# Block 0's out product over four token groups at once, with unit 2 inside it, and the batch rests moved to block 6

## The chip, the core and the metric

The kernel runs on one core of a Trainium2 chip. A core has a matmul engine (TensorE, PE), an elementwise engine (VectorE, DVE), an engine for activations and copies (ScalarE, ACT), a general one (GpSimd, POOL) and a queue engine (SyncE, SP) which here only issues DMA transfers. All five run their own instruction lists in order and wait for one another by semaphores. Matmuls write to PSUM, eight banks of 512 floats in each of 128 partitions; everything else lies in SBUF. The metric is the device time of one execution in microseconds. One execution is also profiled, instruction by instruction; its own time and its span (first to last instruction) are given beside the median.

## What is computed

Chunked attention (chunks of 64 positions, no mask, heads of 64), then a bilinear feed-forward network. Inputs and output are float32.

```python
batch, n_heads, seq, head_dim = (8, 8, 576, 64)
n_tokens, d_model, d_ff = (4608, 512, 1536)
...
q_c = q.reshape(B, H, nc, chunk, D)
k_c = k.reshape(B, H, nc, chunk, D)
v_c = v.reshape(B, H, nc, chunk, D)
scores = scale * np.matmul(q_c, k_c.transpose(0, 1, 2, 4, 3))
scores = scores - np.max(scores, axis=-1, keepdims=True)
attn = np.exp(scores)
attn = attn / (np.sum(attn, axis=-1, keepdims=True) + 1e-09)
out = np.matmul(attn, v_c)
...
x = np.ascontiguousarray(attn_out.transpose(0, 2, 1, 3)).reshape(B * S, H * D)
a = x @ w_a
b = x @ w_b
return (a * b @ w_out).astype(np.float32)
```

## The kernel before, in words

**Blocks and units.** The 4608 tokens are cut into nine blocks (K = 0 to 8) of 512 tokens. A block is two units (u = 2K, 2K + 1) of 256 tokens, that is four chunks of 64. A batch has 576 positions: eight chunks go to a block of their own, and the ninth chunks of all eight batches, the rests, make one more block. `REST` (L51) says which block that is: block 4 before. For the rests two neighbouring chunks come from different batches, so that `runs` (L112) gives two runs of 64 partitions where it gives one of 128 otherwise. Loads (`load_natural`, L119) and stores (`store`, L435) issue one DMA per run: four issues a tensor and unit in place of two, and two a store in place of one.

**Attention of a unit.** q, k, v are loaded into `f32` (three sets), cast to bf16 by POOL (`cast_qk`, `cast_v`; `qkb`, `vb`), and q, k are turned so that the head dimension lies on partitions (`qkT`). For units 4 and up a DMA turns them (`transpose_dma`, L216). For units 2 and 3 PE does: `load_pairs` loads two tokens a row, `cast_pairs` casts, `transpose_pairs` (L190) makes eight transposes for q or k into an F bank, `evacuate_pairs` (L199) copies them out, q by DVE, k by ACT. Then `scores` (32 small matmuls into the two banks `PS`, L234), `expo` (ACT, L245), `sums` (four matmuls of ones with the exponentials, into two F banks, L251), `values` (32 small matmuls into the two banks `PA`, L267), `log_sums` (ACT, L277), `inverse` (ACT, exp of the negative logarithm, L281) and `normalise` (DVE, L286, one for each of the two chunk halves), which writes `xT`. `slot(uv, us)` (L686) issues the sums, values and logarithms of unit uv and the scores of unit us; what follows is put in a list `late`, from which `step()` takes one item before each tile and `drain()` all.

**The network.** A tile `ffn(K, ft)` takes 128 of the 1536 columns of w_b and w_a: four matmuls for b, four for a, into two banks of a ring of four (`F`, by `nextF`, L108); ACT copies b out (L409), DVE multiplies it with a into `ab[ft]` (L410). `us` says which units' columns it takes: both (512 columns) or one (256). The out product of a token group `tg` (128 tokens) is the sum over the twelve ft of ab[ft] times w_out (`out_products`, L420); `out_close` (L428) copies it from PSUM to a buffer `osb`, and `store` writes it out. Blocks 0 and 1 do that; blocks 2 to 8 use a scheme of fewer products (`outs_fast`, L470), which needs sums of w_out halves that POOL makes on the side (`some_sums`). w_out comes in six pieces: `queue_wo(i)` issues the load, `land_wo(i)` casts it on POOL.

**Order.** The order is written out by hand: each engine works through its instructions in the order of the program text, and the DMA issues of SP likewise. Around the change it is:

1. Block 0's twelve tiles (L710 to L729). Meanwhile SP issues the loads of w_out (0 to 5), then of units 2, 3, 4.
2. POOL's casts of w_out, then of units 2 and 3 (L730 to L748).
3. Block 0's out product (L749 to L775): groups 0 and 1 together in two banks, ft by ft; then group 2 in a third bank, with unit 2's transposes after its ft 5, and unit 2's scores and exponentials after it; then group 3, with `slot(2, None)` and unit 3's transposes of q after its ft 4 and those of k after ft 7; at its end unit 3's scores.
4. Casts, w_out sums, turns and loads for the units that follow, and block 0's stores (L777 to L796).
5. Block 1 (L798 to L834). Unit 3's sums and values aren't there yet, so its first seven tiles are done in halves: first unit 2's columns (with `slot(3, None, short=True)` after ft 1), then unit 3's (with unit 4's scores after ft 2); the last five tiles take both. Then its out product.
6. Blocks 2 to 8 in one loop (L837 to L861), with a slot twice a block.

Of the kernel before, what the change touches and what calls it, by code (L numbers as in the profile page):

```python
# [11 lines left out]
def kernel(  # L12
# [10 lines left out]
    nc = tc.nc  # L23
# [14 lines left out]
    NFT = DFF // 128  # L38
    BLK = 512
    NBLK = NTOK // BLK  # L40
# [7 lines left out]
        return sb.tile(shape, dt, name=name)  # L48


    REST = NBLK // 2  # L51
    chunks = []
    for K in range(NBLK):
        if K == REST:
# [7 lines left out]
    PS = pp.tile([128, 2, 512], FP32, name="PS")  # L62
# [45 lines left out]
    def nextF():  # L108
        return ring("f", F)
# [19 lines left out]
    def load_pairs(u, x, src, eng):  # L129

        b, s0 = chunks[4 * u]
        eng.dma_start(
            out=f32[u % NF32][x].rearrange("p (h c) -> p h c", h=H),
            in_=src[b, :, s0:s0 + 256, :].rearrange("h (p r) d -> p h (r d)", r=2),
        )
# [39 lines left out]
    def cast_pairs(u, x, *engs):  # L175
        n = 2 // len(engs)
        for i, eng in enumerate(engs):
            r = slice(n * i, n * i + n)
            copy(
                eng,  # L180
                qkb[u % 2][:, x, :].rearrange("p (r h d) -> p h r d", r=2, h=H)[:, :, r],
                f32[u % NF32][x].rearrange("p (h r d) -> p h r d", h=H, r=2)[:, :, r],
            )
# [3 lines left out]
        for i in range(pieces):  # L187
            copy(eng, vb[u % 3][:, n * i:n * i + n], f32[u % NF32][2][:, n * i:n * i + n])

    def transpose_pairs(u, x):  # L190
        t = nextF()
        for n in range(8):
            c = n * 128
            nc.tensor.transpose(
                t.bitcast(BF16)[:, c:c + 128], qkb[u % 2][:, x, c:c + 128], identity
            )
        return t
# [221 lines left out]
    def out_products(tg, ft, o):  # L419
        nc.tensor.matmul(  # L420
            o,
            ab[ft][:, tg * 128:(tg + 1) * 128],
            wo[ft // 2][:, ft % 2, :],
            start=(ft == 0),
            stop=(ft == NFT - 1),
        )

    def out_close(K, tg, o, now=True):  # L428
        t = ring("o", osb)
        nc.vector.tensor_copy(out=t, in_=o)  # L430
        if now:
            store(K, tg, t)
        return K, tg, t
# [116 lines left out]
    with tc.manual_schedule():  # L550
# [36 lines left out]
        def queue_wo(i):  # L587
            staged["o", i] = load_wo(i, nc.sync)

        def land_wo(i):  # L590
            copy(G, wo[i], staged["o", i].rearrange("p (f c) -> p f c", f=2))
# [69 lines left out]
        def load_unit(u, xs=(0, 1, 2)):  # L661
            for x in once("load", u, xs):
                load_natural(u, x, (q, k, v)[x], nc.sync)

        def cast_unit(u, xs=(0, 1, 2)):
            for x in once("cast", u, xs):
                if x < 2:
                    cast_qk(u, x, G)
                else:
                    cast_v(u, G)  # L670
# [5 lines left out]
        def turn_pairs(u, x, engs):  # L676
            evacuate_pairs(u, x, transpose_pairs(u, x), engs)
# [3 lines left out]
        def drain():  # L681
            while late:
                fn, a = late.pop(0)
                fn(*a)

        def slot(uv, us, pairs=False, short=False):  # L686


            drain()
            if uv is not None:  # L690
                SU = nextF(), nextF()
                sums(uv, SU)
                values(uv)
                log_sums(uv, SU)
                if short:
                    for cl in range(2):
                        late.extend([(inverse, (uv, cl)), (normalise, (uv, cl))])
                else:
                    inverse(uv)
                    late.extend([(normalise, (uv, 0)), (normalise, (uv, 1))])  # L700
            if us is not None:
                scores(us, pairs)
                late.append((expo, (us,)))

        def step():
            if late:
                fn, a = late.pop(0)
                fn(*a)

        for ft in range(1, NFT):  # L710
            ffn(0, ft)
            if ft in (1, 2, 3, 4, 5):
                land_w(ft)
            if ft in (1, 2):
                queue_w(ft + 3)
            if ft == 3:
                for i in range(3):
                    queue_wo(i)
            if ft == 4:
                for i in range(3, 6):  # L720
                    queue_wo(i)
                load_pairs(2, 0, q, nc.sync)
                load_pairs(2, 1, k, nc.sync)
                load_unit(2, (2,))
            if ft == 5:
                load_pairs(3, 0, q, nc.sync)
                load_pairs(3, 1, k, nc.sync)
                load_unit(3, (2,))
                load_unit(4)  # L729
        for i in range(6):  # L730
            land_wo(i)
        wo_sums = [(i, part) for i in range(NP) for part in range(4)]

        def some_sums(n):

            for i, part in wo_sums[:n]:
                sum_wo(i, part, G)
            del wo_sums[:n]

        cast_pairs(2, 0, G)  # L740
        some_sums(1)
        cast_unit(2, (2,))
        cast_pairs(3, 0, G)
        cast_pairs(3, 1, G)
        some_sums(2)
        cast_unit(3, (2,))
        cast_pairs(2, 1, V, A)
        load_unit(5, (0,))  # L748
        o = nextF(), nextF()  # L749
        for ft in range(NFT):  # L750
            for tg in range(2):
                out_products(tg, ft, o[tg])
        stores = [out_close(0, tg, o[tg], False) for tg in range(2)]
        o = nextF()
        for ft in range(NFT):
            out_products(2, ft, o)
            if ft == 5:
                turn_pairs(2, 0, (V,))
                turn_pairs(2, 1, (A,))
        slot(None, 2, True)  # L760
        drain()
        stores.append(out_close(0, 2, o, False))
        o = nextF()
        for ft in range(NFT):
            out_products(3, ft, o)
            if ft == 4:
                slot(2, None)
                turn_pairs(3, 0, (V,))
                drain()
            if ft == 7:  # L770
                nextF()
                turn_pairs(3, 1, (A,))
        stores.append(out_close(0, 3, o, False))
        slot(None, 3, True)
        drain()  # L775

        cast_unit(4, (0,))  # L777
        some_sums(2)
# [6 lines left out]
        for d in stores:  # L785
            store(*d)
        load_unit(6, (0,))
        cast_unit(5, (0,))
        some_sums(3)
        cast_unit(5, (1,))  # L790
# [3 lines left out]
        turn_unit(5)  # L794
        load_unit(6, (1, 2))
        load_unit(7, (0,))  # L796

        for ft in range(7):  # L798
            step()
            ffn(1, ft, (0,))  # L800
            if ft == 1:
                slot(3, None, short=True)
        for ft in range(7):
            step()
            ffn(1, ft, (1,))
            if ft == 2:
                slot(None, 4)
# [6 lines left out]
        load_unit(7, (1, 2))  # L814
        load_unit(8, (0,))
        cast_unit(7, (0, 1))
        for ft in range(7, NFT):
            step()
            ffn(1, ft)
            if ft == 10:  # L820
                slot(4, 5)
# [70 lines left out]
```

## Time and profile before

| | |
|---|---|
| median of 6 runs | 314.98 us (313.9 to 315.84) |
| the profiled execution | 314.69 us, span 312.9 us |
| granted TensorE clock | 1.0 |
| DMA moved over the span | 55.00 MB, mean 176 GB/s |
| HBM read, written | 37.75 MB, 9.44 MB |
| turned q, k (DMA): issues, median to landing | 14, 5.2 us |
| out product of block 0, first matmul | 37.08 us |
| block 1, first matmul | 51.88 us |
| block 1, first tile over both units | 65.48 us |
| block 2, first product of the out step | 110.60 us |

How to read it: engine busy times overlap, so they don't add up to the span. A line of the timeline gives start, duration, engine, source line, operation, what it writes from what, and in brackets how long the engine had stood before it and what ended that. A matmul's duration includes its way through the array, so two that follow each other overlap in the list; the pace is read from starts. Source lines are those of the kernel before. The chain of waits that ended last gives PE 66% of the span, DMA transfers 17% and SP's issues 9%; the part of DMA and SP lies before 107 us:

```
97.50 4.29 DMA f<-in_q_dram
101.79 4.93 DMA qkT<-qkb
106.76 0.45 PE PS L234 x32
107.21 0.32 PE F L398
```

### The profile page before, as it was taken

What the parts mean: (1) busy time and instruction counts of PE and PEld (TensorE: products, weight loads), DVE (VectorE), ACT (ScalarE), POOL (GpSimd) and SP (SyncE); (2) the same over time, 40 slices, a digit from 0 to 9 for tenths busy, and PEclk for the clock granted to TensorE, in tenths of its full rate; (3) what the DMA queues carried; (4) which work ended last, traced back from release to release, by engine and by line L of the source; (5) the groups of instructions that cost most, each with busy time, mean ns of one, the idle gap of its engine ahead of it and who ended that gap; (6) DMA issues with size and microseconds to landing.
All of it is one profiled execution on the core that took longest, in us unless ns stands there. A gap on an engine that the chain in (4) does not pass through costs nothing.

```text
span 312.9 us, 7255 instructions
## 1 busy us (share of the span) xinstructions
PE 301.3 (96%) x2867; PEld 175.9 (56%) x2900; DVE 186.1 (59%) x371; ACT 134.0 (43%) x227; POOL 124.1 (40%) x159
## 2 busy tenths in 40 slices
PE   7799999999999899999999999999999999999995
PEld 3444456864444486447644764476546744674474
DVE  3643344534357755866496749674967475746663
ACT  3833227645246433553255326532644164413220
POOL 2658867977362147402730263016400400040023
PEclk9999999999999999999999999999999999999999
DMA  7999999999988999999799159943700300020003
GB/s 250 295 323 386 399 302 241 226 288 219 238 188 236 191 227 226 231 246 210 220 253 232 38 120 219 245 94 134 136 2 0 128 11 0 3 107 27 2 0 135
DMA packets 146898, 55.00 MB, mean 176 GB/s; under 512 B 126256, under 2 KB 140848, under 8 KB 146864
## 3 DMA queue, kind: packets, MB, share of 16 engines
q1 hardware_dynamic: 145776, 53.49, 68.4%
q10 hardware_dynamic: 1088, 1.05, 1.0%
q8 instruction: 22, 0.36, 0.5%
q14 instruction: 12, 0.10, 0.1%
HBM read 37.75 MB, written 9.44 MB: 151 GB/s over the span
## 4 chain that ended last, share of the span: by engine, by line
PE 66%; DMA 17%; SPq 9%; POOL 2%; issue 2%; ACT 1%; DVE 1%; ACTq 0%; POOLq 0%; DVEq 0%
PE F L398 42%; PE F L479 19%; DMA f<-in_k_dram 5%; SPq L124 5%; DMA wst<-in_moe_w_a_dram 5%; DMA f<-in_v_dram 5%; SPq L154 2%; SPq L216 2%; DMA qkT<-qkb 2%; DMA f<-in_q_dram 1%; POOL vb L169 1%; PE F L251 1%; PE PS L234 1%; PE PA L267 1%; SPq L147 1%
## 5 line engine op out<-in xcount | busy, mean ns | idle before, releaser
L398 PE MATMUL F<-xT,wa 128*128 128x512 bf16 (+1 forms) x460 | 112.4, 366 | 0.7 <-POOL wa L169 0.3
L398 PE MATMUL F<-xT,wb 128*128 128x512 bf16 (+1 forms) x431 | 109.9, 366 | 1.3
L409 ACT CAST bsb<-F 128x512 bf16<-128x512 f32 (+1 forms) x115 | 64.0, 558 | 106.8 <-PE F L398 105.4
L410 DVE TENSOR_TENSOR ab<-F,bsb 128x512 bf16<-128x512 f32 (+1 forms) x115 | 75.3, 656 | 52.8 <-PE F L398 46.7
L398 PEld LDWEIGHTS <-wa 128*128 128x128 bf16 x460 | 44.8, 98 | 49.3 <-POOL wa L169 1.4
L398 PEld LDWEIGHTS <-wb 128*128 128x128 bf16 x460 | 43.4, 98 | 44.7 <-POOL wb L169 0.9
L497 POOL TENSOR_TENSOR part<-part 128x256 f32<-128x256 f32 x14 | 10.1, 724 | 126.9 <-ACT part L523 125.8
L169 POOL CAST qkb<-f 128x1024 bf16<-128x1024 f32 (+1 forms) x35 | 34.8, 1007 | 31.2 <-DMA f<-in_k_dram 16.7
L479 PEld LDWEIGHTS <-wst 128*128 128x128 bf16 x420 | 41.1, 98 | 4.8
L479 PE MATMUL F<-wst 128*128 128x256 bf16 x252 | 33.3, 273 | 0.0
L286 DVE TENSOR_TENSOR xT<-PA,inv 128x512 bf16<-128x512 f32 x32 | 21.8, 685 | 17.1 <-ACT inv L281 17.1
L497 DVE TENSOR_TENSOR osb<-F,part 128x256 f32<-128x256 f32 x56 | 22.3, 420 | 10.9 <-POOL part L497 9.7
L497 POOL TENSOR_TENSOR part<-part,osb 128x256 f32<-128x256 f32 x28 | 19.7, 725 | 11.4 <-DVE osb L497 11.3
L169 POOL CAST vb<-f 128x1024 bf16<-128x1024 f32 (+2 forms) x22 | 19.9, 910 | 7.5 <-DMA f<-in_v_dram 6.4
L479 PE MATMUL F<-wst,ab 128*128 128x256 bf16 x168 | 22.7, 273 | 0.0
L277 ACT ACTIVATE lns<-F 128x512 f32<-128x512 f32 x32 | 17.4, 595 | 10.8 <-PE F L251 10.8
L420 PE MATMUL F<-wo,ab 128*128 128x512 bf16 x92 | 21.3, 379 | 0.4 <-issue 0.3
L467 DVE TENSOR_TENSOR wst<-ab 128x512 bf16<-128x512 bf16 x42 | 20.9, 498 | 0.0
L468 DVE TENSOR_TENSOR wst<-ab 128x512 bf16<-128x512 bf16 x42 | 20.9, 497 | 0.0
L479 PE MATMUL F<-wo,wst 128*128 128x256 bf16 x168 | 20.6, 273 | 0.0
L245 ACT ACTIVATE E<-PS 128x1024 bf16<-128x1024 f32 (+1 forms) x20 | 18.8, 942 | 3.7 <-PE PS L234 2.5
L497 DVE TENSOR_TENSOR part<-F,part 128x256 f32<-128x256 f32 x15 | 6.4, 424 | 21.4 <-POOL part L497 21.4
(52 smaller groups left out, 195.9 us busy)
## 6 DMA issues: line engine op xcount, KB each, us to landing
out_dram<-osb SPq DMA_DIRECT2D x31, 256.0 KB, 2.9
f<-in_q_dram SPq DMA_DIRECT2D x28, 256.0 KB, 4.1
f<-in_v_dram SPq DMA_DIRECT2D x28, 256.0 KB, 4.4
f<-in_k_dram SPq DMA_DIRECT2D x24, 256.0 KB, 4.3
wst<-in_moe_w_out_dram SPq DMA_DIRECT2D x6, 512.0 KB, 8.6
f<-in_v_dram SPq DMA_DIRECT2D x16, 128.0 KB, 3.1
wst<-in_moe_w_b_dram SPq DMA_DIRECT2D x4, 512.0 KB, 7.5
wst<-in_moe_w_a_dram SPq DMA_DIRECT2D x4, 512.0 KB, 7.8
```

The costliest lines, as they stand in the source:

```text
L169: eng.tensor_copy(out=out, in_=in_)
L245: nc.scalar.activation(out=e[:, :, s], in_=PS[:, :, s], func=AF.Exp, scale=scale)
L277: nc.scalar.activation(out=lns[:, cl, :], in_=SU[cl], func=AF.Ln)
L286: nc.vector.tensor_tensor(out=x.rearrange("p m (g c t) -> p c g m t", g=2, c=2)[:, cl], in0=PA[:, cl, :].rearrange(shape, g=2, m=4), in1=i ...
L398: nc.tensor.matmul(bank[:, 0:n], w[ft // 2][ft % 2][:, kt, :], x[:, kt, us[0] * 256:us[0] * 256 + n], start=(kt == 0), stop=(kt == NKT - 1),)
L409: nc.scalar.copy(out=bT[:, 0:n], in_=banks[0][:, 0:n])
L410: nc.vector.tensor_tensor(out=ab[ft][:, us[0] * 256:us[0] * 256 + n], in0=banks[1][:, 0:n], in1=bT[:, 0:n], op=MULT)
L420: nc.tensor.matmul(o, ab[ft][:, tg * 128:(tg + 1) * 128], wo[ft // 2][:, ft % 2, :], start=(ft == 0), stop=(ft == NFT - 1),)
L467: nc.vector.tensor_tensor(out=y[:, 0:2], in0=a[:, 0:2], in1=a[:, 2:4], op=ADD)
L468: nc.vector.tensor_tensor(out=y[:, 2:4], in0=a[:, 1:3], in1=a[:, 0:4:3], op=SUB)
L479: nc.tensor.matmul(o, a(i)[:, c:c + 128], b(i), start=(i == 0), stop=(i == NP - 1))
L497: eng.tensor_tensor(out=out, in0=in0, in1=in1, op=op)
```

## The change

- **Rests.** `REST` becomes block 6. Units 8 and 9 are then ordinary chunks, units 12 and 13 hold the rests.
- **Loads.** During block 0's tiles, SP issues w_out pieces 0 to 3, then unit 2's q and k, then w_out piece 4, unit 2's v, w_out piece 5, and then unit 3 as before.
- **Casts.** POOL casts w_out 0 to 3, unit 2's q, w_out 4, unit 2's v, w_out 5, then unit 3; unit 2's k is cast by DVE and ACT, a half each, as before. One w_out sum fewer is made in this stretch and one more later.
- **Out product of block 0.** All four groups run together in the four F banks: ft 0 to 9 with the four groups side by side, and ft 10 and 11 group by group. Unit 2 sits inside it and uses the score banks `PS` in place of F banks: its transposes after ft 5, its scores and exponentials after ft 7, its sums (into `PS`), values, logarithms, inverses and normalises after ft 9. The four sums are copied out at the end, groups 0 and 2 by DVE, 1 and 3 by ACT.
- **Unit 3** moves into block 1's half tiles: its transposes after ft 1, its scores after ft 3, its `slot(3, None, short=True)` after ft 5. Ten tiles are done in halves in place of seven.
- **POOL's and SP's lists** for units 4 to 7 keep their order; the casts of unit 5 now stand in the text behind the first halves.

```diff
-    REST = NBLK // 2
+    REST = NBLK - 3
...
-    def transpose_pairs(u, x):
-        t = nextF()
+    def transpose_pairs(u, x, t=None):
+        t = nextF() if t is None else t
...
-    def out_close(K, tg, o, now=True):
+    def out_close(K, tg, o, now=True, eng=None):
         t = ring("o", osb)
-        nc.vector.tensor_copy(out=t, in_=o)
+        copy(eng or nc.vector, t, o)
...
             if ft == 3:
-                for i in range(3):
-                    queue_wo(i)
-            if ft == 4:
-                for i in range(3, 6):
+                for i in range(4):
                     queue_wo(i)
                 load_pairs(2, 0, q, nc.sync)
                 load_pairs(2, 1, k, nc.sync)
+            if ft == 4:
+                queue_wo(4)
                 load_unit(2, (2,))
+                queue_wo(5)
...
-        for i in range(6):
-            land_wo(i)
...
+        for i in range(4):
+            land_wo(i)
         cast_pairs(2, 0, G)
+        cast_pairs(2, 1, V, A)
+        land_wo(4)
+        cast_unit(2, (2,))
+        land_wo(5)
+        cast_pairs(3, 0, G)
         some_sums(1)
-        cast_unit(2, (2,))
-        cast_pairs(3, 0, G)
         cast_pairs(3, 1, G)
-        some_sums(2)
+        some_sums(1)
         cast_unit(3, (2,))
-        cast_pairs(2, 1, V, A)
         load_unit(5, (0,))
-        o = nextF(), nextF()
-        for ft in range(NFT):
-            for tg in range(2):
-                out_products(tg, ft, o[tg])
-        stores = [out_close(0, tg, o[tg], False) for tg in range(2)]
-        o = nextF()
-        for ft in range(NFT):
-            out_products(2, ft, o)
-            if ft == 5:
-                turn_pairs(2, 0, (V,))
-                turn_pairs(2, 1, (A,))
-        slot(None, 2, True)
-        drain()
-        stores.append(out_close(0, 2, o, False))
-        o = nextF()
-        for ft in range(NFT):
-            out_products(3, ft, o)
-            if ft == 4:
-                slot(2, None)
-                turn_pairs(3, 0, (V,))
-                drain()
-            if ft == 7:
-                nextF()
-                turn_pairs(3, 1, (A,))
-        stores.append(out_close(0, 3, o, False))
-        slot(None, 3, True)
-        drain()
+
+        o = [nextF() for _ in range(4)]
+        for fts in [(ft,) for ft in range(NFT - 2)] + [(NFT - 2, NFT - 1)]:
+            for tg in range(4):
+                for ft in fts:
+                    out_products(tg, ft, o[tg])
+            if fts == (5,):
+                t = [transpose_pairs(2, x, PS[:, x, :]) for x in range(2)]
+                evacuate_pairs(2, 0, t[0], (V,))
+                evacuate_pairs(2, 1, t[1], (A,))
+            if fts == (7,):
+                scores(2, True)
+                expo(2)
+            if fts == (9,):
+                SU = PS[:, 0, :], PS[:, 1, :]
+                sums(2, SU)
+                values(2)
+                log_sums(2, SU)
+                for cl in range(2):
+                    inverse(2, cl)
+                    normalise(2, cl)
+        stores = [out_close(0, tg, o[tg], False, (V, A)[tg % 2]) for tg in range(4)]
...
         load_unit(6, (0,))
+
+        for ft in range(10):
+            step()
+            ffn(1, ft, (0,))
+            if ft == 1:
+                turn_pairs(3, 0, (V,))
+                turn_pairs(3, 1, (A,))
+            if ft == 3:
+                slot(None, 3, True)
+            if ft == 5:
+                slot(3, None, short=True)
         cast_unit(5, (0,))
...
-        for ft in range(7):
-            step()
-            ffn(1, ft, (0,))
-            if ft == 1:
-                slot(3, None, short=True)
-        for ft in range(7):
+        for ft in range(10):
             step()
             ffn(1, ft, (1,))
             if ft == 2:
...
-        for ft in range(7, NFT):
+        for ft in range(10, NFT):
             step()
             ffn(1, ft)
```

## The prediction

> **What bounds the kernel now.** I read the page's busy table first, then the waits of the matmul engine, then its stretches and the timeline around block 0's out product, and last the DMA queue. The busy table:
>
> ```profile
> PE 301.3 (96%) x2867; PEld 175.9 (56%) x2900; DVE 186.1 (59%) x371; ACT 134.0 (43%) x227; POOL 124.1 (40%) x159
> ```
>
> PE sets the time: a change is worth what it takes from PE's idle time, or what work it adds to PE. Between 36 and 112 us, where the edits act, PE's list of waits (engine and line, what it waited for, total us, times, longest) is short:
>
> ```profile
> PE PS L234 <- DMA qkT<-qkb: 1.0, 1, 1.0
> PE F L420 <- issue: 0.3, 2, 0.2
> ```
>
> The first is 0.99 us at 106.76, where the scores of unit 8 wait for their turned q, k. The three stretches are: out product of block 0; half-unit tiles of block 1; the rest up to block 2's out product (columns: stretch, its us, then each engine's busy us and instructions, clock, DMA share, GB/s):
>
> ```profile
> 37.08:51.88 14.80, 14.35 (x179) 7.77 (x181) 6.32 (x10) 5.82 (x9) 10.66 (x11) 1.00 1.10 295
> 51.88:65.48 13.60, 13.60 (x184) 11.68 (x181) 6.97 (x16) 8.71 (x20) 12.33 (x14) 1.00 1.08 242
> 65.48:110.60 45.12, 43.71 (x452) 20.79 (x456) 25.36 (x44) 21.30 (x34) 22.38 (x24) 1.00 0.97 221
> ```
>
> The granted clock is 1.00 throughout. The timeline of the first stretch (start, us, engine, line; in brackets the idle time before):
>
> ```profile
> 37.35 0.69 DVE L410 TENSOR_TENSOR ab<-F,bsb 128x512 bf16<-128x512 f32 x1 [1.03 <-PE F L398]
> ...
> 46.11 0.64 PE L234 MATMUL PS<-qkT 64*64 64x64 bf16 x32
> ...
> 47.88 0.41 PE L251 MATMUL F<-E,ones 64*64 64x512 bf16 x4
> ...
> 48.32 1.09 ACT L277 ACTIVATE lns<-F 128x512 f32<-128x512 f32 x2 [0.50 <-PE F L251]
> ...
> 48.49 0.62 PE L194 MATMUL F<-identity,qkb 128*128 128x128 bf16 x8
> ...
> 49.44 1.06 ACT L281 ACTIVATE inv<-lns 128x1024 f32<-128x1024 f32 x1
> ...
> 50.53 1.29 DVE L286 TENSOR_TENSOR xT<-PA,inv 128x512 bf16<-128x512 f32 x2 [0.64 <-ACT inv L281]
> ...
> 51.74 0.68 DVE L430 COPY osb<-F 128x512 f32<-128x512 f32 x1
> 51.88 0.60 PE L398 MATMUL F<-xT,wb 128*128 128x256 bf16 x4
> ```
>
> From unit 2's sums (47.88) to its normalised x (51.82) and block 1's first tile (51.88) the chain PE, ACT, ACT, DVE takes 4.00 us. Now PE spends that time on out products, unit 3's transposes and unit 3's scores.
>
> **Part 1: all four token groups at once.** PE does the same 48 out products (30 of them from 37.08 to 43.55: 0.2157 each). The four sums take all four F banks. The fourth is the bank of block 0's last product, which DVE leaves at 38.04 (37.35 + 0.69). PE wants it after three products, at 37.08 + 0.65 = 37.73. A PE start follows a DVE end by 0.06 (51.82 to 51.88), so PE stands until 38.10: 0.37 lost, with all of PE's queue behind it. Then 21 products (4.53) end ft 5 at 42.63.
>
> Unit 2's k needs its casts by then. It landed at 42.45 behind six out weights; those land 1.27 apart (their casts start at 36.87, 38.14, 39.42), so with two of them behind it, it lands near 39.9, and the slower cast (DVE, 1.10) ends at 41.0: 1.6 us of cover, and each us beyond that would cost PE one. The last out weight goes behind q, k and v of unit 2, whose v cast began at 44.34; with its own cast (1.04) it is ready near 45.4, wanted at ft 10 near 48.3: cover 2.9.
>
> The 16 transposes go to the score banks. Eight take 0.46 and 0.44 (48.49 to 48.95, 49.60 to 50.04): 0.90, to 43.53. Today their second half also waits 0.24 for an F bank; that goes. Two ft (8 products, 1.73) end at 45.26. ACT starts its evacuation 0.64 after the second eight begin (44.28, 44.92) and takes 1.07: ready at 44.79, so no wait, with 0.47 cover. Scores: today 0.80 from 46.11 to the next product; between 0.64 and 0.80 I take 0.70, to 45.96. Two more ft end at 47.69; exp (starts 0.69 after the scores, lasts 1.02) is done at 46.97. So unit 2's sums start at 47.69, against 47.88.
>
> From there the chain differs in two places. The inverse is split, so that the first normalise starts after 0.44 + 1.09 + 0.03 + 0.63 + 0.03 = 2.22, and both end at 3.51. But on DVE the copy of group 0's sum stands behind both normalises, and block 1's first tile takes that bank: the copy starts at 3.45 (instructions overlap by some 0.07) and ends at 4.13, so PE may go on at 4.19: 51.88. That is the same moment as before, to the hundredth by chance; the bounds are 0.3 either way (score price, where waits round). In between PE has only sums and values (0.61, 47.88 to 48.49) and 8 products (1.73), done at 50.03: **1.85 us of PE idle**. ACT's two copies (after the second inverse, 50.5 to 51.7) and DVE's second free the other banks in time.
>
> A rule weighs on this. The 1.85 would be 0.67 smaller (4.19 - 3.52) with a free bank; the rest is the chain to x. The Trainium skill (Perfetto Trace Analysis, Identifying Performance Opportunities) reads repeated gaps on the engine that should be saturated as possibly too little PSUM for the next tile; by it alone the whole 1.85 would be the banks' price and this stretch would end at 50.03 with a spare one, by the rows at 51.2.
>
> **Part 2: unit 3 moves behind it.** What PE did for unit 3 before 51.88 now comes inside block 1's half tiles, where PE has nothing idle (13.60 of 13.60). Transposes: 0.90. Scores: the plain ones cost 0.38 (61.60 to the next tile at 61.98), the paired ones 0.64 busy: 0.50 taken. Sum +1.40 (1.28 to 1.54). Here their evacuation is hidden: ft 2 and 3 (1.75) follow, ACT needs 0.19 + 1.07.
>
> The Trainium skill (PSUM — Partial Sum Buffer, Specifications) says that a non-contiguous access pattern slows matmuls significantly, without a figure. The paired scores write every second element; the rows above agree in direction (0.64 against 0.45 busy for 32). By the rule the upper price would hold, total +0.14; by the rows the middle.
>
> Half tiles: a half ft takes 0.875 (two of 0.4375: 54.84, 55.27, 55.71), a whole one 1.73 (65.48, 67.21); three more ft in halves cost 3 x 0.02 = +0.06.
>
> New waits in the halves, from 51.88: ft 0, 1 end at 53.63; transposes 54.53; ft 2, 3 56.28; scores 56.78; exp on ACT 56.98 to 58.00; ft 4, 5 58.53. ACT's copy for ft 4 stands behind exp and ends at 58.30, DVE's product at 58.72, and only then is the second bank for unit 3's sums free: PE, there at 58.65, waits 0.13. After the sums, x of unit 3 was ready 4.75 later (53.71 to 58.46) with five ft to cover it, and PE was there at 58.84, 0.32 in hand after the 0.06. Now only four ft (6 to 9) lie in between: 0.32 - 0.875 = -0.55. I take a wait of 0.50 (0.2 to 0.6, as exact interleaving on ACT decides). Sum +0.63.
>
> **Part 3: rests of batches as block 6.** Units 8, 9 load in pieces of 64 partitions today (4 issues a tensor), afterwards in 2; units 12, 13 the other way round. The DMA queue of SP:
>
> ```profile
> 89.06 3.64 SPq L124 DMA_DIRECT2D f<-in_k_dram  x4
> 92.75 2.67 SPq L124 DMA_DIRECT2D f<-in_v_dram  x4
> 95.46 2.68 SPq L124 DMA_DIRECT2D f<-in_q_dram  x4
> 98.23 3.45 SPq L438 DMA_DIRECT2D out_dram<-osb  x4
> 101.79 2.88 SPq L216 DMA_TRANSPOSE qkT<-qkb  x1
> ```
>
> It runs without a pause, and the turn of unit 8 stands at its end: issued at 101.79, landed 4.93 later at 106.72, PE at 106.76. Two issues take 1.19 to 1.25 where nothing holds them up. Four tensors (q 2.90) of 11.9 us shrink to some 5 to 8 (where the DMA engines hold them back, two took 2.1): the turn lands 4 or more earlier, and PE comes 2 later. The wait of 0.99 goes either way. For units 12 and 13 each tensor's issue is longer by at most 1.5; unit 12's turn is issued at 154.68 and its scores run at 169.04, unit 13's 162.37 and 187.9: cover over 9 us even after landing. POOL's casts of unit 13 (155.58) stand before nothing urgent, as its next add is at 177. Price 0; were the cover gone, 4.5 (three tensors of 1.5). Splitting the stores of block 6 instead of block 4 costs as much as it saves.
>
> **Sum**: out stretch 0.0 (-0.3 to +0.3), unit 3's work +1.40, halves +0.06, waits +0.63, unit 8's wait -0.99: **+1.10**. The profiled execution took 314.69 for a span of 312.9, 0.29 under the median 314.98. So 315.8 on its own base and **316.1** on the median's.
>
> **Rivals.**
> (a) Not slower: the load chain. Its place is the scores of unit 8; its price is the wait W that the median run pays there. The change costs 2.09 without it, so from W = 1.15 on (2.09 - 0.94) the kernel isn't slower by 0.3%. For: the SP chain runs without slack for 24 us, and six runs spread from 313.9 to 315.84. If that spread is W's, the changed kernel, which doesn't wait there, stands at 314.69 + 1.10 = 315.8 (+0.8) whatever W was. Against: the weights at 20 to 25 us may spread too. Chance 0.27. For a gain over 0.3% W would have to be above 3.0, or the 1.85 idle be absent; the x chain forbids the latter: 0.08.
> (b) Heavier: out weights or k come late. For: DMA share is 1.10 in this stretch, so nothing catches up. Against: covers of 2.9 and 1.6. A slip of 3 us in k gives 1.4 more: 317.5. Chance 0.1.
> (c) The wait isn't removed but moves to units 12, 13: needs a slip over 9 us; +2.09 + wait, 317.1 or more. Chance 0.03.
> The forecast itself: 0.52.
>
> **How the numbers follow.** Adding low ends (-0.3, -0.12, -0.3) gives +0.4, high ends (+0.3, +0.14, +0.1) +1.6: 315.1 to 316.9 by both bases; taken to 315.0 and 317.2 for (a) and (b). 0.3% (0.94 us) is about what a measurement of this kernel can tell from no change. Slower: 0.52 + 0.1 + 0.03 = 0.65. Within: the 0.27 of (a), which takes in the forecast's own low end. Faster: 0.08.
>
> **What would show it.** Right: a PE gap near 0.37 before the fourth out product (37.7); a gap of 1.6 to 2.1 before block 1's first tile, ended by DVE's copy of group 0's sum; 16 transposes and 32 scores inside the half tiles; a gap of 0.2 to 0.6 before the second halves, ended by DVE's normalise; no wait for unit 8's turn. Wrong: block 1's first tile before 51.4, or a wait for a cast of k or an out weight, or unit 8's wait still there.

## The result, and the profile after

Timed side by side, the changed kernel took 316.56 us (median of 35 runs, 315.7 to 318.36), the kernel before 315.37 us (72 runs, 313.85 to 317.9). The ratio is 1.0038, with a 95% interval of 1.0026 to 1.0050: slower by 1.2 us (0.8 to 1.6). The forecast was +1.10 us with a range of 315.0 to 317.2. The profiled execution of the changed kernel took 317.09 us, 2.4 more than that of the kernel before; half of that is no work of the change, as the stretches show. (One profile among the experiments, that of run 6, had a mean granted clock of 0.949; its distances are not compared.)

The busy table of the changed kernel: PE has 0.7 us more of busy time in a span that is 2.4 longer.

```profile
PE 302.0 (96%) x2891; PEld 178.8 (57%) x2924; DVE 185.1 (59%) x372; ACT 135.5 (43%) x233; POOL 124.0 (39%) x159
```

The stretches (columns as before the change: stretch, its us, busy us and instructions of PE, PEld, DVE, ACT, POOL, clock, DMA share, GB/s), cut at points that both kernels pass (what lies between two cuts differs where the change moved it): the start up to the first out product of block 0, block 0's out product, block 1's tiles up to the tenth ft, the rest up to the first product of block 2's out step, and from there to the end. First the kernel before, cut like the other:

```profile
0.00:37.08 37.08, 32.24 (x271) 15.24 (x274) 16.11 (x27) 16.16 (x26) 23.14 (x44) 1.00 1.00 328
...
51.88:70.67 18.79, 18.74 (x208) 14.04 (x206) 8.78 (x19) 10.61 (x23) 16.53 (x19) 1.00 1.08 251
70.67:110.60 39.93, 38.57 (x428) 18.43 (x432) 23.55 (x41) 19.40 (x30) 18.18 (x20) 1.00 0.95 214
110.60:312.90 202.30, 197.42 (x1791) 120.41 (x1811) 131.30 (x275) 82.04 (x140) 55.57 (x68) 1.00 0.53 124
```

and the changed kernel:

```profile
0.00:38.37 38.37, 32.88 (x270) 15.88 (x273) 15.98 (x27) 16.26 (x26) 23.03 (x43) 0.96 0.99 316
38.37:53.30 14.93, 12.71 (x130) 6.45 (x132) 3.75 (x7) 5.80 (x10) 10.18 (x10) 1.00 1.05 285
53.30:74.19 20.89, 20.55 (x277) 17.63 (x277) 10.18 (x23) 11.94 (x28) 16.64 (x19) 1.00 1.16 231
74.19:113.05 38.86, 38.44 (x429) 18.44 (x433) 23.02 (x41) 19.43 (x31) 18.68 (x20) 1.00 1.09 245
113.05:315.30 202.25, 197.41 (x1791) 120.38 (x1811) 132.16 (x276) 82.04 (x140) 55.50 (x67) 1.00 0.49 120
```

Read the second column. Out product: 14.80 to 14.93, +0.13. Tiles: 18.79 to 20.89, +2.10. Rest: 39.93 to 38.86, -1.07. End: -0.05. Together +1.1, close to the 1.2 between the medians. The start is 1.29 longer too, but it is not the change's: block 0's first tile was already 0.92 late (16.51 against 15.59), before the first DMA issue that the edit moves (at 26 us). The granted clock of that stretch was 0.96 against 1.00, but starts of 38.17 and 38.38 came at 1.00 too (runs 5 and 4). A second profile of either kernel, below, puts it the other way round. So the kernels are compared by the distance from block 0's first out product to block 2's first out product: 73.52 before (37.08 to 110.60), 74.68 after (38.37 to 113.05).

PE's list of waits from 30 to 115 us in the changed kernel (engine and line, what it waited for, total us, times, longest):

```profile
PE F L398 <- DVE osb L169: 1.8, 1, 1.8
PE F L398 <- DVE xT L286: 0.3, 1, 0.3
PE F L420 <- DVE ab L410: 0.2, 1, 0.2
PE PS L234 <- ACT qkT L167: 0.2, 1, 0.2
PE F L420 <- issue: 0.2, 1, 0.2
```

The wait for the turned q, k of unit 8 is gone; five others have come, the longest ahead of block 1. Its timeline (start, us, engine, line, operation; in brackets the idle time before it):

```profile
38.37 0.81 PE L420 MATMUL F<-wo,ab 128*128 128x512 bf16 x3
...
38.64 0.69 DVE L410 TENSOR_TENSOR ab<-F,bsb 128x512 bf16<-128x512 f32 x1 [1.03 <-PE F L398]
39.39 4.69 PE L420 MATMUL F<-wo,ab 128*128 128x512 bf16 x20 [0.20 <-DVE ab L410]
...
45.01 0.69 DVE L169 COPY qkT<-PS 128x1024 bf16<-128x1024 bf16 x1 [3.08 <-PE PS L194]
45.74 1.07 ACT L167 COPY qkT<-PS 128x512 bf16<-128x512 bf16 x2 [3.69 <-DVE qkT L169]
...
46.86 0.64 PE L234 MATMUL PS<-qkT 64*64 64x64 bf16 x32 [0.16 <-ACT qkT L167]
47.44 1.90 PE L420 MATMUL F<-wo,ab 128*128 128x512 bf16 x7
...
49.27 0.41 PE L251 MATMUL PS<-E,ones 64*64 64x512 bf16 x4
...
51.36 1.29 DVE L286 TENSOR_TENSOR xT<-PA,inv 128x512 bf16<-128x512 f32 x2 [5.66 <-PE F L420]
...
52.57 1.28 DVE L169 COPY osb<-F 128x512 f32<-128x512 f32 x2
53.30 0.60 PE L398 MATMUL F<-xT,wb 128*128 128x256 bf16 x4 [1.75 <-DVE osb L169]
```

Three things are to be seen. The fourth group's product waits for DVE's last product of block 0: three products would end at 39.02, the next starts at 39.39. ACT's copy of the turned k waits for DVE's copy of the turned q (45.70), and PE's scores for ACT. And the first tile of block 1 follows DVE's copy of group 0's sum, which stands behind both normalises.

### The profile page after: what moved, and what is told of

It reads as the page before. It is cut to its first block, busy times and chain, and to the rows that moved or that the text cites. A ratio compares the mean times of both kernels' runs of the same rounds, so it can differ in the third digit from the quotient of the medians.

```text
span 315.3 us, 7318 instructions
## 1 busy us (share of the span) xinstructions
PE 302.0 (96%) x2891; PEld 178.8 (57%) x2924; DVE 185.1 (59%) x372; ACT 135.5 (43%) x233; POOL 124.0 (39%) x159
## 4 chain that ended last, share of the span: by engine, by line
PE 86%; DMA 4%; SPq 3%; DVE 2%; issue 1%; ACT 1%; POOL 1%; ACTq 0%; POOLq 0%; DVEq 0%
PE F L398 56%; PE F L479 19%; PE F L420 6%; DMA wst<-in_moe_w_a_dram 2%; DMA f<-in_k_dram 2%; SPq L154 2%; PE PS L234 2%; PE F L251 2%; PE PA L267 1%; DVE xT L286 1%; SPq L147 1%; DVE ab L410 0%; POOL part L497 0%; ACT qkT L167 0%; ACTq L140 0%
## 5 line engine op out<-in xcount | busy, mean ns | idle before, releaser
L398 PEld LDWEIGHTS <-wa 128*128 128x128 bf16 x472 | 46.0, 98 | 48.8 <-POOL wa L169 2.0
L398 PEld LDWEIGHTS <-wb 128*128 128x128 bf16 x472 | 44.7, 98 | 45.4 <-issue 1.8
L467 DVE TENSOR_TENSOR wst<-ab 128x512 bf16<-128x512 bf16 x42 | 21.7, 517 | 0.0
L468 DVE TENSOR_TENSOR wst<-ab 128x512 bf16<-128x512 bf16 x42 | 20.9, 497 | 0.0
L277 ACT ACTIVATE lns<-F 128x512 f32<-128x512 f32 x30 | 16.3, 595 | 10.3 <-PE F L251 10.3
```

Of the source, the lines that this page charges most:

```text
L277: nc.scalar.activation(out=lns[:, cl, :], in_=SU[cl], func=AF.Ln)
L398: nc.tensor.matmul(bank[:, 0:n], w[ft // 2][ft % 2][:, kt, :], x[:, kt, us[0] * 256:us[0] * 256 + n], start=(kt == 0), stop=(kt == NKT - 1),)
L467: nc.vector.tensor_tensor(out=y[:, 0:2], in0=a[:, 0:2], in1=a[:, 2:4], op=ADD)
L468: nc.vector.tensor_tensor(out=y[:, 2:4], in0=a[:, 1:3], in1=a[:, 0:4:3], op=SUB)
```

## The experiments

Each was timed in turns with the kernel before, in five rounds; runs 5, 8 and 11 were executed and profiled once only. Times are given against the kernel before; two versions are compared by their profiles. "Distance" is the one above; one matmul less or more in a record moves it by nothing, as it goes by starts.

**1. The rests alone.** The kernel before with one edit:

```diff
-    REST = NBLK // 2
+    REST = NBLK - 3
```

> The kernel before, with only the rests of the batches put into block 6. Theory: units 8 and 9 load in half the DMA issues, the turn of unit 8 lands well before PE asks for it, and the 0.99 us that PE stood at the scores of unit 8 go; nothing else changes, so the time is 0.9 to 1.1 us under the kernel before (ratio 0.9966 to 0.9972), and PE's list of waits between 36 and 112 us has no wait for the turned q, k. Rival (the wait W at unit 8 is larger in the usual run than in the profiled one): 1.3 us or more under, ratio 0.996 or less. Rival (the wait moves to units 12, 13): no gain, and a wait for their turned q, k between 155 and 190 us.

Ratio 0.9984 (0.9966 to 1.0003): -0.5 us, between -1.1 and +0.1. PE's waits from 30 to 200 us:

```profile
PE F L420 <- issue: 0.3, 2, 0.2
```

The wait is gone, none came at units 12, 13, and the distance is 72.38 (38.35 to 110.73), 1.14 under the first profile of the kernel before. So it is shown that the move takes the wait away, while the time alone can't tell 1.1 from nothing.

**2. The rests back in block 4, in the changed kernel** (the same line the other way).

> The changed kernel with the rests back in block 4. Theory: PE comes to the scores of unit 8 some 2.1 us later than in the kernel before, after the turn has landed, so the wait is absent or under 0.2 us without the move too, and the time is that of the changed kernel within 0.3 us (+1.0 to +1.5 us on the kernel before). Rival (the move of the rests is what removes the wait in the changed kernel): the wait of 1 us is back, +2.0 to +2.4 us.

1.0046 (1.0024 to 1.0067), +1.4 us, and a distance of 74.67 (38.02 to 112.69), that of the changed kernel within 0.01. No wait for unit 8. So in the changed kernel the move of the rests is worth nothing that this profile or the time shows: PE, which comes later, doesn't have to wait for the load chain either way.

**3. The loads and casts in the old order, in the changed kernel** (but for POOL's first w_out sum, which stays behind the cast of unit 3's q).

```diff
-                for i in range(4):
+                for i in range(3):
                     queue_wo(i)
-                load_pairs(2, 0, q, nc.sync)
-                load_pairs(2, 1, k, nc.sync)
             if ft == 4:
-                queue_wo(4)
+                for i in range(3, 6):
+                    queue_wo(i)
+                load_pairs(2, 0, q, nc.sync)
+                load_pairs(2, 1, k, nc.sync)
                 load_unit(2, (2,))
-                queue_wo(5)
...
```

> The changed kernel with all six out weights loaded and cast ahead of unit 2's q, k, as in the kernel before. Theory: k then lands about 2.4 us later, its casts end 0.4 to 1 us after PE has finished ft 5, and PE waits that long ahead of the transposes: +0.4 to +1.0 us on the changed kernel, +1.6 to +2.2 us on the kernel before. Rival (the new order of the loads is what costs, by slowing the first 37 us, which were 1.29 us longer in the profile of the changed kernel): 1 us or more under the changed kernel, about the time of the kernel before.

1.0046 (1.0025 to 1.0066), +1.4 us; distance 74.89, 0.21 over the changed kernel. k's casts began 5.7 us after the first out product (43.34, 37.63) and 3.06 after it in the changed kernel (41.43, 38.37): 2.65 later, near the 2.4 expected. But the wait between the two halves of the transposes was only 0.28, not 0.4 to 1, since DVE's cast took 0.43, not the 1.10 that the profile of before gave it (run 11 says why):

```profile
43.89 0.45 PEld L194 LDWEIGHTS <-qkb 128*128 128x128 bf16 x8 [0.28 <-DVE qkb L169]
```

So the theory had the place right and the size too large. The rival falls: the time is not under that of the changed kernel, and the start, 37.63, lies between that kernel's two (38.37 and 37.19).

**4. Group 0's copy ahead of the normalises, in the changed kernel.**

```diff
                 for cl in range(2):
                     inverse(2, cl)
-                    normalise(2, cl)
-        stores = [out_close(0, tg, o[tg], False, (V, A)[tg % 2]) for tg in range(4)]
+        stores = [out_close(0, 0, o[0], False, V)]
+        for cl in range(2):
+            normalise(2, cl)
+        stores += [out_close(0, tg, o[tg], False, (V, A)[tg % 2]) for tg in range(1, 4)]
```

> The changed kernel with one line moved: DVE copies group 0's sum out before the two normalises of unit 2 in place of after them. Theory: block 1's first tile then waits only for x; the stand ahead of it shrinks from 1.75 us to about 1.15, 0.6 us under the changed kernel, +0.5 to +0.7 us on the kernel before. Rival (the stand is that of the chain to x alone and the bank is beside the point): no change, +1.0 to +1.4 us on the kernel before.

1.0015 (0.9987 to 1.0042), +0.5 us; distance 74.01 (38.38 to 112.39), 0.67 less. The wait ahead of block 1 in its timeline:

```profile
52.71 0.60 PE L398 MATMUL F<-xT,wb 128*128 128x256 bf16 x4 [1.16 <-DVE xT L286]
```

The stand is 1.16 in place of 1.75, and what ends it is the normalise. So of 1.75 us the bank holds 0.6 and the chain to x the rest. The profile shows this; the time (-0.4 to +1.3 us) is too uncertain to tell it.

**5. The kernel before again** (profiled once, no edit).

> The kernel before once more, for a second profile of it. In five profiles taken since, the out product of block 0 began at 37.6 to 38.4 us, against 37.08 in the first profile of the kernel before. Theory: the start of the out product wanders by a microsecond whatever the kernel, and the wait at the scores of unit 8 takes up part of that, as its turn hangs on the load chain and not on PE: with an out product that begins at 38 or later the wait is 0 to 0.5 us and the distance from the first out product to the first product of block 2's out step is 72.5 to 73.1 us. Rival: the wait belongs to the order of loads and is 0.9 to 1.1 us again, with a distance of 73.4 to 73.6 us.

The theory fell, and the rival was too low. PE's waits from 30 to 200 us:

```profile
PE PS L234 <- DMA qkT<-qkb: 1.3, 1, 1.3
PE F L194 <- DVE osb L430: 0.8, 1, 0.8
```

The distance is 74.66 (38.17 to 112.83), 1.14 more than in the first profile. Of that, 1.06 are waits: 1.27 at unit 8 in place of 0.99, and 0.78 at unit 2's transposes, whose bank waits for copies that stand behind DVE's late cast of k. Both hang on loads, the second also on POOL, whose sum made that cast last 1.11 (run 11). So in the kernel before the price of the load waits changes from run to run (0.99 and 2.05 in two profiles).

**6. Unit 3's transposes into the stand**, on top of run 4:

```diff
+        t = [transpose_pairs(3, x, PS[:, x, :]) for x in range(2)]
         stores += [out_close(0, tg, o[tg], False, (V, A)[tg % 2]) for tg in range(1, 4)]
+        evacuate_pairs(3, 0, t[0], (V,))
...
             if ft == 1:
-                turn_pairs(3, 0, (V,))
-                turn_pairs(3, 1, (A,))
+                evacuate_pairs(3, 1, t[1], (A,))
```

> The run with the copy of group 0 first, and besides unit 3's transposes taken out of block 1's tiles and put behind the last out product, into the score banks, where PE stands for 1.16 us. Theory: the stand shrinks to 0.2 to 0.4 us and the transposes cost nothing: 0.85 to 0.9 us under the run with the copy first, the distance from the first out product to block 2's out step 73.1 us (74.0 there), and -0.4 to +0.1 us on the kernel before. Rival (what fills the stand delays the chain to x by as much): no gain on the run with the copy first.

0.9998 (0.9972 to 1.0025), -0.1 us (-0.9 to +0.8): inside what the theory said, though the interval alone doesn't rule the rival out. PE's list of waits has no entry ahead of block 1 any more, and the tiles no transposes.

**7. No gaps**: on top of run 6, unit 2's steps one ft earlier, ft 0 and 1 by group, eleven tiles in halves.

```diff
-        for fts in [(ft,) for ft in range(NFT - 2)] + [(NFT - 2, NFT - 1)]:
+        for fts in [(0, 1)] + [(ft,) for ft in range(2, NFT - 3)] + [(9, 10, 11)]:
...
-            if fts == (5,):
+            if fts == (4,):
...
-            if fts == (7,):
+            if fts == (6,):
...
-            if fts == (9,):
+            if fts == (8,):
...
-        for ft in range(10):
+        for ft in range(11):
...
+            if ft == 10:
+                slot(4, 5)
...
-            if ft == 10:
-                slot(4, 5)
```

> As the run that fills the gap, and unit 2's three steps one ft earlier, ft 0 and 1 group by group, and eleven tiles in halves in place of ten. Theory: the stands of 0.37 (fourth bank), of 0.2 to 0.4 (ahead of block 1) and of 0.34 (second halves) go too: a distance of 72.0 to 72.4 us, 0.6 to 1.3 us under the kernel before, ratio 0.996 to 0.998. Rival (k of unit 2 then lands too late for the earlier transposes): a wait of 0.3 us or more for its cast, and no gain on the run that fills the gap.

0.9984 (0.9954 to 1.0014), distance 73.76 (38.26 to 112.02) in place of 72.0 to 72.4. The stands that it was to remove are gone (block 1 begins at 52.01, 13.75 after the first out product, 14.93 in the changed kernel), but the gain met a new wait, named by neither theory, at the scores of unit 5:

```profile
75.07 0.45 PE L234 MATMUL PS<-qkT 64*64 64x64 bf16 x32 [1.06 <-DMA qkT<-qkb]
```

In the changed kernel the turn of unit 5 is issued at 70.81 and lands 5.7 later, at 76.5; PE asks for it at 76.61. Its cover (the time between landing and use) is 0.1 us there, so a PE that comes a microsecond earlier waits.

**8. Unit 3's scores written contiguously** (profiled once, changed kernel; unit 3's tokens come out in another order within a chunk).

```diff
-                            o = o.rearrange("p (t r) -> p r t", r=2)
+                            if u != 3:
+                                o = o.rearrange("p (t r) -> p r t", r=2)
                             qt = tp[j * 64:j * 64 + 64, m, :, n:n + 32]
```

> The changed kernel, with the scores of unit 3 written to contiguous elements of the score banks; they are read from q as before, so that unit 3's tokens come out in another order within a chunk. Theory (the strided write to PSUM is what makes the paired scores dearer than the plain ones, 0.58 against 0.37 us for 32): 0.37 to 0.40 us from the scores of unit 3 to the next tile. Rival (the strided reading of q costs it): 0.55 to 0.60 us as before.

Its timeline (lines move down by one in this kernel), with unit 2's scores, which are written as before, above unit 3's:

```profile
45.90 0.64 PE L235 MATMUL PS<-qkT 64*64 64x64 bf16 x32 [0.16 <-ACT qkT L167]
46.47 1.90 PE L421 MATMUL F<-wo,ab 128*128 128x512 bf16 x8
...
56.83 0.45 PE L235 MATMUL PS<-qkT 64*64 64x64 bf16 x32
57.21 0.61 PE L399 MATMUL F<-xT,wb 128*128 128x256 bf16 x4
```

0.38 from unit 3's scores to the next tile, against 0.58 in the changed kernel (57.79 to 58.37) and 0.57 for unit 2's here. The strided write into PSUM costs the 0.2; the strided read of q, which stayed, costs nothing, as plain scores also take 0.38 (61.60 to 61.98 in the kernel before).

**9. Unit 5's scores later**, on top of run 7: they go behind block 1's first out group, its sums behind the second.

```diff
-                slot(4, 5)
+                slot(4, None)
...
             if tg == 0:
+                slot(None, 5)
+            if tg == 1:
                 slot(5, None)
```

> As the run without gaps, with the scores of unit 5 moved behind block 1's first out group and its sums behind the second, because in that run PE stood 1.06 us at the scores of unit 5 for their turned q, k. Theory: the load chain sets when these land, and 2.6 us more of work ahead of them covers it: no such wait, a distance from the first out product to block 2's out step of 72.4 to 72.9 us (73.76 there), and 0.6 to 1.6 us under the kernel before (ratio 0.995 to 0.998). Rival (the chain then holds up the next unit instead): a wait of 0.5 us or more at the scores of unit 6, 7 or 8, and a distance of 73.2 us or more.

0.9989 (0.9962 to 1.0016), distance 73.86 (38.08 to 111.94). The wait at unit 5 is gone, but not the time, and the rival named the wrong place: PE now waits for DVE's products in block 2. The timeline of DVE and POOL there:

```profile
92.68 1.32 POOL L457 TENSOR_TENSOR wst<-wst 128x512 bf16<-128x512 f32 x1
92.79 1.49 DVE L467 TENSOR_TENSOR wst<-ab 128x512 bf16<-128x512 bf16 x1
93.96 2.45 POOL L460 TENSOR_TENSOR wst<-wst 128x256 bf16<-128x256 f32 x3
94.20 0.94 DVE L468 TENSOR_TENSOR wst<-ab 128x512 bf16<-128x512 bf16 x1
...
96.36 2.08 POOL L169 CAST qkb<-f 128x1024 bf16<-128x1024 f32 x2
...
97.46 1.25 DVE L467 TENSOR_TENSOR wst<-ab 128x512 bf16<-128x512 bf16 x1
...
99.70 1.02 PE L398 MATMUL F<-xT,wa 128*128 128x512 bf16 x4 [1.00 <-DVE ab L410]
```

L467 is the same add everywhere; its median is 0.42 us. Beside POOL's sums of w_out it takes 1.49, and beside POOL's casts of unit 8's q and k, which follow those sums, 1.25. DVE falls behind, and PE stands 0.32 and 1.00 us for its products. Five POOL sums had ended up beside block 2's first tiles, as PE comes there earlier than before. (The expectation of run 12 puts the 1.25 down to a sum and calls 0.42 the time elsewhere; the trace shows a cast, and 1.25 again beside POOL's casts in later blocks, in the kernel before too.)

**10. The changed kernel again.**

> The changed kernel once more, on the chip and beside the runs of the version with later scores, and for a second profile. Theory: its distance from the first out product to block 2's out step is 74.7 us again (74.6 to 74.8), as nothing on the way waits for a load, while the start of the out product may be anywhere from 37.1 to 38.4 us; +0.8 to +1.6 us on the kernel before. Rival (the distance wanders with the loads as that of the kernel before, 73.5 and 74.7): outside 74.4 to 75.0.

1.0027 (0.9999 to 1.0055), +0.9 us; distance 74.61 (37.19 to 111.80), and the same five waits. The start is 37.19 here and 38.37 in the first profile, so a start 1.2 us longer or shorter says nothing of the kernel. The changed kernel's distance was the same in its two profiles and in run 2 (74.68, 74.61, 74.67), the other's was not (73.52, 74.66). Three profiles don't prove it steady: run 11, which moves one POOL sum, has 75.56, with a wait for unit 5's turn that these three don't have; run 8, whose scores are 0.2 shorter, has 74.85, with 0.27 at a product of DVE.

**11. POOL's first sum beside DVE's cast** (profiled once, changed kernel).

```diff
         cast_pairs(2, 1, V, A)
+        some_sums(1)
         land_wo(4)
...
         cast_pairs(3, 0, G)
-        some_sums(1)
         cast_pairs(3, 1, G)
```

> The changed kernel with POOL's first sum of w_out halves (1.27 us) moved ahead of the cast of the fifth out weight, so that POOL adds while DVE casts its half of unit 2's k. In the profiles with the casts in the order of the kernel before, POOL ran that sum then and DVE's cast took 1.07 to 1.11 us; in the others POOL stood and it took 0.43. Theory: DVE's cast can't run beside POOL's sum: it takes 0.9 to 1.2 us and ends some 0.3 us after the sum. Rival (the cast is slow for the late landing of k or its order on DVE): 0.43 us.

```profile
41.01 1.27 POOL L457 TENSOR_TENSOR wst<-wst 128x512 bf16<-128x512 f32 x1
41.37 0.62 ACT L167 CAST qkb<-f 128x512 bf16<-128x512 f32 x1 [3.06 <-DMA f<-in_k_dram]
41.44 1.12 DVE L169 CAST qkb<-f 128x512 bf16<-128x512 f32 x1 [2.09 <-DMA f<-in_k_dram]
```

1.12 us, and it ends 0.28 after POOL's sum (42.56, 42.28). In the kernel before it ended 0.28 after it too (43.62, 43.34). The theory holds: with the cast otherwise unchanged, POOL's sum beside it makes it end just after the sum. (The one time of this run, 318.12 us, has a wait of 0.81 us at unit 5's scores, whose cover was 0.1 in the changed kernel.)

**12. POOL's last sums earlier**, on top of run 9: five sums go ahead of the casts of unit 7's q and k, where POOL stands for loads.

```diff
+        some_sums(24)
         cast_unit(7, (0, 1))
...
         cast_unit(7, (2,))
-        some_sums(24)
```

> As the run with unit 5's scores later, with POOL's last five sums of w_out halves (some 4.1 us) moved ahead of its casts of unit 7's q and k, into time in which POOL stands for loads. In the run with later scores they ran from 92 to 96 us beside DVE's first sums of block 2, whose 512-element adds took 1.25 and 1.49 us there against 0.42 elsewhere, and PE then stood 0.32 and 1.00 us for DVE's products. Theory: without POOL's sums beside them DVE's adds take 0.4 to 0.5 us and both stands go: a distance from the first out product to block 2's out step of 72.4 to 72.8 us (73.86 there), 0.8 to 1.8 us under the kernel before (ratio 0.994 to 0.9975). Rival (DVE is late in block 2 because unit 5's normalises come later, not for POOL): the stands stay and the distance is 73.5 us or more.

0.9974 (0.9951 to 0.9997): 0.8 us under the kernel before (0.1 to 1.5), the one version here whose interval against the kernel before lies below 1. The same adds in block 2:

```profile
92.12 0.42 DVE L467 TENSOR_TENSOR wst<-ab 128x512 bf16<-128x512 bf16 x1
92.45 0.42 DVE L468 TENSOR_TENSOR wst<-ab 128x512 bf16<-128x512 bf16 x1
```

Both stands for DVE's products are gone. The distance is 73.04 (37.57 to 110.61), over the 72.4 to 72.8 expected; five small waits of 0.2 to 0.3 are left, one of them for turned q, k. So the rival falls, though POOL's casts moved with its sums, and no run parts the two.

Set beside run 1, this is little: there one line, the move of the rests, gave a distance of 72.38 and a ratio of 0.9984, and the two intervals overlap. That the joint out product, even with the mends of runs 4 to 12, is worth anything beside that line is not shown.

## Why the prediction was right

**The out stretch, forecast 0.0, measured +0.13.** The 0.37 ahead of the fourth product is exact (39.02 to 39.39). k landed with 1.9 us of cover (casts done at 42.05, transposes at 43.92), 1.6 forecast (DVE's cast took 0.43, not 1.10, as no sum of POOL ran beside it); the last out weight with 3.0 (cast done at 46.90, ft 10 at 49.87), 2.9 forecast. The stand ahead of block 1 was 1.75 for 1.85. One step failed: ACT's copy of the turned k was put at 0.64 after the second eight transposes, by the row of the kernel before, with 0.47 of cover. In the changed kernel it waits for DVE's copy of q (45.01 to 45.70, ACT at 45.74). The likely reason is in the program: both copies read the score banks, which are one tile, where F banks are two. No run tests it, but unit 3's transposes, in F banks, agree: there ACT's copy starts at 56.14 while DVE's runs from 55.70 to 56.39. So the scores began 0.31 later than worked out. That the stretch still came to +0.13 is in part luck: two terms that were put too high paid it back, scores 0.58 for 0.70, and sums to first tile 4.03 for 4.19; two ft took 1.83 for 1.73 (0.31 - 0.12 - 0.16 + 0.10).

**Unit 3 and the halves, forecast +2.09, measured +2.10.** Transposes 0.89 (55.05 to 55.94) for 0.90; scores 0.58 for 0.50; the second halves waited from 64.47, where the last product would have ended (64.03 + 0.44), to 64.96, 0.49 for 0.50:

```profile
55.05 1.06 PE L194 MATMUL F<-identity,qkb 128*128 128x128 bf16 x16
...
55.94 0.60 PE L398 MATMUL F<-xT,wb 128*128 128x256 bf16 x4
...
57.79 0.64 PE L234 MATMUL PS<-qkT 64*64 64x64 bf16 x32
...
58.37 0.61 PE L398 MATMUL F<-xT,wb 128*128 128x256 bf16 x4
...
64.22 0.68 DVE L286 TENSOR_TENSOR xT<-PA,inv 128x512 bf16<-128x512 f32 x1
...
64.96 0.61 PE L398 MATMUL F<-xT,wb 128*128 128x256 bf16 x4 [0.34 <-DVE xT L286]
```

The normalise ends at 64.90 and the tile follows 0.06 later. (The list's 0.34 is less, since a matmul's recorded end has its way through the array in it.) The wait of 0.13 for the second sums bank didn't show: sums and values took 0.67 as before. With 0.06 for the halves the terms come to 2.02; the other 0.08 is spread over gaps too small for the list.

**Unit 8, forecast -0.99, measured -1.07.** The wait went, and in run 2 it goes without the move of the rests too, as the prediction said. The turn's lead was mis-sized: it was issued at 101.01 and landed 5.7 later, which is 2.1 and 1.3 earlier than before when measured from the first out product, not 4 or more. The four tensors took 7.2 us, as estimated, and from unit 8's q to the turn the queue took 4.25 less than in the kernel before; but it came to unit 8's q 2.2 later (48.8 after the first out product, 46.6 in the kernel before), a shift that the prediction didn't count. It stayed without effect, as PE asked at 109.18.

**The rivals.** (a) had the right cause in the kernel before: load waits that change from run to run, 0.99 and 2.05 in two profiles. So it is partly luck that a sum made on one profile came within 0.1 of the timed difference. By distance the changed kernel is 1.16 behind the first profile of the kernel before and level with the second; the first, at 314.69, lies nearer the median of 315.37 than the second, at 316.88. How large the wait is in the usual execution is not shown; run 1 gives 0.5 (-0.1 to 1.1) for taking it away. (b) and (c) didn't occur: PE's waits up to 200 us, in run 1 and in the changed kernel, have none at units 12, 13.

**The bank rule.** Run 4 gives the bank 0.6 of the 1.75 and the chain to x 1.16; the rows gave 0.67 (0.62, had the 0.06 from DVE's end to PE's start been put behind x too). The rule alone would have given the bank all of it.

**The range.** The high ends of the terms add up to 316.6 on the median's base (314.98 + 1.6), not to the 316.9 of the prediction. The bound of 317.2 was set above either.

## What to carry to other kernels

When a product takes all banks of a ring at once, look at both edges: the last user of each bank ahead of it, and in which order on its engine the bank is copied out behind it. Work taken out of a stall and put where an engine is full costs its whole price (here 0.89 for the transposes and 0.58 for the scores). And when the engine that sets the time is made faster, its loads are asked for earlier (runs 7 and 9 lost much of their gain to that, or to what it put side by side): work out the cover of the next loads before counting the gain, and compare stretches between two like points, since the start wanders by more than the effect.

## What the runs showed of the hardware

DVE and POOL hold each other up. DVE's cast of 128x512 to bf16 took 0.43 us in the profiles where POOL stood and 1.07 to 1.12 beside POOL's sum, ending 0.28 after it each time; DVE's add of two bf16 tensors of 128x512 took 0.42 alone, 0.94 to 1.49 beside POOL's sums and 1.25 beside POOL's casts, and it too ended 0.28 after the instruction of POOL that it met (run 9: 94.28 and 94.00). POOL is held up as well: its cast of 128x1024 took 1.04 alone and 1.22 to 1.23 beside DVE's adds (at 160.05 in the changed kernel). The Trainium skill (SBUF — State Buffer, Who interferes with whom) describes a pair of ports shared by the two engines: in VectorE's two-port modes the one that issues first holds the pair for its whole instruction while the other is blocked, and an add with both inputs in SBUF contends with GpSimd's reads. The numbers agree with a block rather than a slower pace: DVE ended 0.28 after POOL whether it had begun 0.11 after POOL's start (the add of run 9) or 0.45 (the cast of the kernel before).

Writing the 64-column scores to every second element of PSUM cost 0.2 us in 32 matmuls (0.58 against 0.38, run 8), reading q in two strides nothing.

The start up to block 0's out product took 37.1 to 38.4 us in the profiles, whatever the kernel.
